# Transposes in 64x64 tiles for about half of the work, PSUM as four pairs for any step, output in halves, and no second loads

## The chip, the core and the metric

The kernel runs on one core of a Trainium2 chip. The metric is the device time of one execution in microseconds (us), as the median of several runs. Beside the timed runs there is one profiled execution; every duration below that is not a median comes from it. The engines are TensorE (PE, with its weight loads as PEld), VectorE (DVE), ScalarE (ACT), GpSimd (POOL) and SyncE (SP, which issues most DMAs).

## What is computed

Sigmoid attention over 8 batches, 12 heads, 448 positions and a head width of 64, and then a token-mixing MLP over the attention's output. The reference, cut to what matters:

```python
scores = scale * np.matmul(q, k.transpose(0, 1, 3, 2)) - np.log(S)     # S = 448
attn = 1.0 / (1.0 + np.exp(-scores))
attn_out = np.matmul(attn, v)                                         # [8, 12, 448, 64]
x = attn_out.transpose(0, 2, 1, 3).reshape(B, S, H * D)               # [8, 448, 768]
wq = x @ w_q                                                          # [8, 448, 64]
wk = x @ w_k
W_tok = 1/np.sqrt(64) * np.einsum('bsd,btd->bst', wq, wk)
mixed = np.einsum('bst,btd->bsd', W_tok, x)
out = np.maximum(mixed, 0.0) @ w_out                                  # [8, 448, 768]
```

All inputs and the output are float32; the kernel computes in bfloat16 with float32 accumulation.

## The kernel before

**The unit of work** is a quad: four heads of one batch, three quads to a batch, 24 in all. A quad's q, k and v (448 KB each) are loaded as [128 partitions, 2, 7*64]: a partition holds seven consecutive positions of a head, and `i` from 0 to 6 counts them. GpSimd casts them to bfloat16 (`cast1`, L131).

**Letters.** All work of PE after the start is written out as a string, `PLAN` (L464), one letter for a step; PE, and with it DVE and ACT, runs the steps in exactly this order. Each row of the string belongs to one quad's seven score steps.

- `q`, `k` (`tr`, L149): the transposition of a quad's q or k. For most quads PE does it: seven whole-array 128x128 transposes (L161) into one PSUM bank and a copy by DVE (L165). For quads 16 to 22 (`TWICE`) DVE does it with a 32x32 block transpose (L154). That needs another layout, for which `load1` (L107) loads most of the data twice, with four DMAs of 216 KB in place of one of 448 KB (tiles qb and kb).
- `S` (`scores`, L170): four 64x64 matmuls of 448 columns that run side by side in the array's four quarters, then one sigmoid of 128x896 on ACT (L179).
- `P` (`values`, L185): four 64x64 matmuls that add one seventh of the values to PSUM; after seven, DVE copies the result out (L201).
- `x` (`tr_x`, L206): eight whole-array transposes of the attention's output (L213) and a copy by DVE (L218).
- `W`, `N`, `U`, `M`: the mixing MLP of a batch. `W` (L228) is one of six matmuls with w_q and w_k; `N` (L244) four whole-array transposes; `U` (L252) eight 128x64 matmuls; `M` (L270) four 64x64 matmuls and a relu, on DVE, or on ACT for `m`.
- `O` (`out_chunk`, L292): six 128x128 matmuls of 384 columns that make half of an output block, and a copy on DVE, or on ACT for `o`; every second one issues the block's stores.
- `K`: the rest of the first quad's k.

**PSUM** has eight banks of 2 KB per partition. Three pairs of banks (`free2`) serve `S`, `P` and `M`; two single banks (`free1`) serve everything else. Each list is used first in, first out.

**Loads.** `ORDER` (L377) is the order in which SP issues the loads and GpSimd casts them. `pump_loads` (L394) issues a load when the buffer that it needs has been cast from (three buffers per tensor, two of the double kind), and `pump` (L409) casts when the cast's own buffer is free. The SP queue also carries the output's stores, in program order.

**The tail.** From the last score step on, what remains is 7 P, 6 W, 2 x, N, U, 6 M and 15 O; copies are then divided over DVE and ACT and stores over SP and ACT.

Of the kernel before, what the change touches and what calls it, by code (L numbers as in the profile page):

```python
# [16 lines left out]
def kernel(  # L17
# [19 lines left out]
    P = 128  # L37
# [27 lines left out]
    ps_f = pool("ps_f", 1, space=bass.MemoryType.PSUM)  # L65

    free2 = ["a", "b", "c"]
    free1 = ["d", "e"]

    def bank2(name):  # L70
        n = free2.pop(0)
        return n, ps_q.tile([P, 2, 512], F32, tag=n, name=name)

    def bank(shape, dtype, name):
        n = free1.pop(0)
        return n, ps_f.tile(shape, dtype, tag=n, name=name)
# [3 lines left out]
    wqk32 = singles.tile([P, NC, P], F32, name="wqk32")  # L80
# [4 lines left out]
    zeros = singles.tile([P, P], BF16)  # L85
# [16 lines left out]
    TWICE = {'q': (16, 17, 18, 19, 20, 21, 22), 'k': (16, 17, 18, 19, 20, 21, 22)}  # L102
# [3 lines left out]

    def load1(n, nm, eng):  # L107
        u, j = quads[n]
        if n in TWICE.get(nm, ()):
            t = p_lb.tile([P, 2, 14 * HD], F32, tag=nm + "b32", name=nm + "b32")  # L110
            for g in range(2):
                src = SRC[nm][u, 4 * j + 2 * g : 4 * j + 2 * g + 2].rearrange(
                    "h (p r) d -> p h (r d)", r=14
                )
                for dh in range(2):
                    r0 = 64 * g + 32 * dh
                    eng.dma_start(  # L117
                        out=t[r0 : r0 + 32, :, 0 : 13 * HD + 32],
                        in_=src[:, :, 32 * dh : 32 * dh + 13 * HD + 32],
                    )  # L120
        else:
            t = p_ld.tile([P, 2, NI * HD], F32, tag=nm + "32", name=nm + "32")
            eng.dma_start(  # L123
                out=t,
                in_=SRC[nm][u, 4 * j : 4 * j + 4].rearrange(
                    "(g h) (p i) d -> (h p) g (i d)", g=2, i=NI
                ),
            )
        ld[nm, n] = t

    def cast1(n, nm, eng):  # L131
        if n in TWICE.get(nm, ()):
# [5 lines left out]
        else:  # L138
            p = p_v16 if nm == "v" else p_c16
            t16 = p.tile([P, NI, 2, HD], BF16, tag=nm + "16", name=nm + "16")  # L140
            eng.tensor_copy(  # L141
                out=t16.rearrange("p i b d -> p b i d"),
                in_=ld.pop((nm, n)).rearrange("p b (i d) -> p b i d", i=NI),
            )
        ld[nm + "16", n] = t16

    qk = {}

    def tr(n, nm):  # L149
        t16 = ld.pop((nm + "16", n))  # L150
        t = p_qk.tile([P, 2, NI, NP], BF16, tag=nm + "t", name=nm + "t")
        qk[nm, n] = t
        if n in TWICE.get(nm, ()):
            nc.vector.transpose(  # L154
                out=t.rearrange("p h i n -> p (h i n)").bitcast(F32),
# [3 lines left out]
        fb, ps = bank([P, NI, 2, NP], BF16, "pt" + nm)  # L159
        for i in range(NI):  # L160
            nc.tensor.transpose(  # L161
                ps[:, i].rearrange("p h n -> p (h n)"),
                t16[:, i].rearrange("p b d -> p (b d)"), ident16,
            )
        nc.vector.tensor_copy(out=t, in_=ps.rearrange("p i h n -> p h i n"))  # L165
        free1.append(fb)
# [3 lines left out]
    def scores(n, i):  # L170
        fb, sc = bank2("sc")
        for g in range(2):
            for h in range(2):
                nc.tensor.matmul(  # L174
                    sc[HALF[h], g, 0:S], qk["k", n][HALF[g], h, i, :],
                    qk["q", n][HALF[g], h].rearrange("p i n -> p (i n)"), start=True, stop=True,
# [3 lines left out]
        free2.append(fb)  # L180
# [4 lines left out]
    def values(n, i, tail):  # L185
        u, j = quads[n]
        if i == 0:
            pv[n] = bank2("pv")
        fb, ps = pv[n]
# [6 lines left out]
        if i == NI - 1:  # L196
# [5 lines left out]
            free2.append(fb)  # L202
# [3 lines left out]
    def tr_x(n, tail):  # L206
# [3 lines left out]
        fb, ps = bank([P, 4, 2, 2, HD], BF16, "px")  # L210
        for h in range(2):
            for m in range(4):
                nc.tensor.transpose(  # L213
                    ps[:, m, :, h], xt(u, j)[:, h, m * P : (m + 1) * P], ident16
                )
        for g in range(2) if tail else (slice(0, 2),):
            w = slice(2 * j * P, 2 * (j + 1) * P) if not tail else slice((2 * j + g) * P, (2 * j + g + 1) * P)
            COPY["s" if tail and g else "v"](  # L218
                out=xns[u][:, :, w],
                in_=ps[:, :, g].rearrange("p m h d -> p m (h d)")  # L220
                if tail else ps.rearrange("p m g h d -> p m (g h d)"),
            )
        free1.append(fb)
# [4 lines left out]
    def mlp_wqk(u, c, tail):  # L228
        if c == 0:
            pw[u] = bank([P, S], F32, "pw")  # L230
        fb, ps = pw[u]
# [3 lines left out]
        if c == NC - 1:  # L235
# [6 lines left out]
            free1.append(fb)  # L242

    def mlp_wkn(u):  # L244
        fb, ps = bank([P, 4, P], BF16, "pk")
        for m in range(4):
            nc.tensor.transpose(ps[:, m], wqks[u % 2][:, m * P : (m + 1) * P], ident16)
        wkn[u] = p_one.tile([P, 4, DH], BF16, tag="wkn", name="wkn")
        nc.vector.tensor_copy(out=wkn[u], in_=ps[:, :, 64:128])
        free1.append(fb)  # L250

    def mlp_tmp(u, act):  # L252
        tmps[u] = p_one.tile([P, NB], BF16, tag="tmp", name="tmp")
        fb, ps = bank([P, NB], F32, "pt")
# [7 lines left out]
        free1.append(fb)  # L262
# [7 lines left out]
    def mlp_mix(u, c, act, tail):  # L270
        if c == 0 and u % 2 == 0:
            mxs[u // 2] = [p_mx.tile([P, 2, 2, S], BF16, tag=f"mx{n}", name="mx") for n in range(NC // 2)]
        fb, ps = bank2("pm")
# [13 lines left out]
        free2.append(fb)  # L287
# [3 lines left out]

    def out_chunk(act, tail):  # L292
        w, m, nb = chunks.pop(0)
        if nb == 0:
# [3 lines left out]
        def block(ps, w0, w1):  # L298
            for c in range(NC):
# [14 lines left out]
        fb, ps = bank([P, NB], F32, "po")  # L314
        if tail and w == NU // 2 - 1 and not chunks:
            h = NB // 2
            block(ps[:, 0:h], NB, NB + h)
            nc.vector.tensor_copy(out=o[:, NB : NB + h], in_=ps[:, 0:h])
            fb2, ps2 = bank2("po")
            block(ps2[:, 0, 0:h], NB + h, D)  # L320
            nc.scalar.copy(out=o[:, NB + h :], in_=ps2[:, 0, 0:h])
            store(slice(NB, NB + h))
            store(slice(NB + h, D))
            return
        block(ps, nb * NB, (nb + 1) * NB)
        COPY["s" if act else "v"](out=o[:, nb * NB : (nb + 1) * NB], in_=ps)  # L326
        free1.append(fb)
# [6 lines left out]
    def load_weights():  # L334
        for x, w in enumerate((moe_w_q, moe_w_k)):
            nc.sync.dma_start(
                out=wqk32[:, :, 64 * x : 64 * x + 64], in_=w.rearrange("(c p) n -> p c n", p=P)
# [20 lines left out]
    nc.vector.memset(zeros, 0.0)  # L358
    nc.vector.memset(bias_t, attn_bias)
    nc.gpsimd.memset(ident, 0.0)  # L360
# [6 lines left out]
    fb, ps = bank2("pwarm")  # L367
    for _ in range(32):
        nc.tensor.matmul(ps[:, 0, 0:P], zeros, zeros, start=True, stop=True)
    free2.append(fb)  # L370
    for t in xts:
        nc.vector.memset(t[:, :, S:], 0.0)
    for t in wqks:
# [4 lines left out]
        "v0 q1 k1 v1 k2 q2 q3 k3 q4 k4 v2 k5 k6 w0 k7 v3 "  # L378
        "w1 q5 q6 k8 v4 w2 q7 w3 v5 w4 k9 q8 v6 q9 w5 w6 "
        "v7 q10 k10 v8 v9 q11 k11 q12 v10 k12 v11 q13 k13 k14 q14 q15 "  # L380
        "v12 q16 k15 v13 v14 q17 k16 v15 k17 q18 k18 q19 v16 k19 v17 k20 "
        "k21 v18 v19 v20 v21 q20 q21 q22 v22 q23 k22 k23 v23 "
# [3 lines left out]
    BACK = {}  # L386
    for nm in "qkv":
        mine = {True: [], False: []}
        for n in range(N):
            kind = n in TWICE.get(nm, ())  # L390
            BACK[nm, n] = (kind, list(mine[kind]))
            mine[kind].append(n)

    def pump_loads():  # L394
        while len(loaded) < len(ORDER):
            nm, n = ORDER[len(loaded)]
            if nm == "w":
                if n >= 3 and ("w", n - 2) not in cast:
                    break
                load_wout(n - 1) if n else load_weights()  # L400
            else:
                kind, before = BACK[nm, n]
                back = 2 if kind else 3
# [154 lines left out]
```

## Time and profile before

| | us |
|---|---|
| median of 3 runs (205.08 to 206.51) | 205.62 |
| the profiled execution | 204.95 |
| its span, from the first to the last instruction | 203.2 |
| PE busy | 192.2 |
| ACT busy | 171.2 |
| DVE busy | 123.1 |
| POOL busy | 80.3 |
| sigmoids (L179), 168 of 1.016 | 156.1 busy |
| output matmuls (L300), 342 | 61.8 busy |
| DMA | 53.13 MB, mean 262 GB/s |
| loads of the double kind | 56 issues of 216 KB |

Busy time is the union of the instructions' spans. A matmul's span holds its way through the array, so that spans of following matmuls overlap; what a matmul costs is the distance to the start of the next. An engine's idle time costs nothing where another engine sets the pace. In a line of the profile `sc<-qt,kt` says that the tile sc is written from qt and kt, `128x896 bf16` are partitions, elements and type, and `x8` is the number of instructions merged into the line.

### The profile page before, as it was taken

To read this page: it belongs to the slowest core of one execution; us is meant where nothing else is said; L and a number is where in the kernel's file an instruction comes from. 1 tells how busy PE (TensorE), PEld (TensorE's weight loads), DVE (VectorE), ACT (ScalarE), POOL (GpSimd) and SP (SyncE) were. 2 spreads that over 40 slices of the span, in tenths; PEclk is the share of its full clock that TensorE was granted. 3 is DMA by queue.
4 is the path that set the end of the run, shared out by engine and by line. 5 is a ranking of instruction groups with operands and counts; after the bars stand their busy time and mean duration, and the time that the engine had idled before them with its cause. 6 is when DMAs were issued, how large, how long until landed. Compare 5 with 4: busy or idle time off the path is not lost.

```text
span 203.2 us, 5863 instructions
## 1 busy us (share of the span) xinstructions
PE 192.2 (95%) x2388; PEld 108.6 (53%) x2388; DVE 123.1 (61%) x196; ACT 171.2 (84%) x200; POOL 80.3 (40%) x95
## 2 busy tenths in 40 slices
PE   7669999999999999999999999999999899999991
PEld 7335545545556566555656555545455455555561
DVE  2226655866498567668777776858777654471230
ACT  4796999999989999889999999898998959974511
POOL 1577688676416624217642442511632600000000
PEclk9996999999999999999999999999999999999999
DMA  6999999899998999999999999999899933303575
GB/s 193 374 383 375 325 380 355 245 395 382 380 381 258 331 254 317 223 265 261 247 223 285 256 282 236 367 260 252 258 287 214 345 90 78 80 3 97 152 203 168
DMA packets 27786, 53.13 MB, mean 262 GB/s; under 512 B 4464, under 2 KB 19952, under 8 KB 27760
## 3 DMA queue, kind: packets, MB, share of 16 engines
q1 hardware_dynamic: 26960, 51.19, 85.9%
q10 hardware_dynamic: 800, 1.57, 2.1%
q8 instruction: 18, 0.29, 0.6%
q14 instruction: 8, 0.07, 0.1%
HBM read 41.75 MB, written 11.01 MB: 260 GB/s over the span
## 4 chain that ended last, share of the span: by engine, by line
DMA 41%; PE 31%; SPq 8%; ACT 8%; issue 4%; POOL 4%; DVE 1%; ACTq 1%; POOLq 0%
DMA qb<-in_q_dram 17%; DMA kb<-in_k_dram 12%; PE po L300 11%; PE sc L174 6%; ACT at L179 6%; SPq L117 5%; PE pv L192 5%; DMA q<-in_q_dram 4%; DMA out_dram<-o 4%; DMA v<-in_v_dram 4%; SPq L123 2%; PE pw L232 2%; PE ptk L161 2%; POOL k L134 2%; PE pt L257 2%
## 5 line engine op out<-in xcount | busy, mean ns | idle before, releaser
L179 ACT ACTIVATE at<-sc,bias_t 128x896 bf16<-128x896 f32 x168 | 156.1, 1016 | 13.6 <-PE sc L174 12.7
L300 PE MATMUL po<-wout,mx 128*128 128x384 bf16 (+1 forms) x342 | 61.8, 324 | 0.5 <-ACT o L326 0.3
L174 PE MATMUL sc<-qt,kt 64*64 64x448 bf16 x672 | 57.3, 363 | 2.4 <-DVE kt L451 1.0
L192 PE MATMUL pv<-at,v 64*64 64x448 bf16 x672 | 43.2, 353 | 0.7 <-POOL v L141 0.6
L300 PEld LDWEIGHTS <-mx 128*128 128x128 bf16 x342 | 30.9, 98 | 24.0 <-issue 7.0
L174 PEld LDWEIGHTS <-kt 64*64 64x64 bf16 x672 | 22.1, 104 | 24.3 <-issue 13.0
L201 DVE CAST xt<-pv 128x896 bf16<-128x896 f32 x23 | 25.0, 1088 | 16.1 <-PE pv L192 15.9
L326 DVE COPY o<-po 128x384 f32<-128x384 f32 x39 | 21.7, 556 | 16.9 <-PE po L300 11.8
L141 POOL CAST v<-v 128x896 bf16<-128x896 f32 x24 | 22.4, 934 | 15.2 <-PE pv L192 7.8
L268 DVE TENSOR_SCALAR mx<-pm 128x896 bf16<-128x896 f32 (+1 forms) x24 | 23.0, 969 | 7.2 <-PE pm L277 7.1
L192 PEld LDWEIGHTS <-v 64*64 64x64 bf16 x672 | 20.2, 107 | 12.3 <-issue 2.0
L218 DVE COPY xn<-px 128x1024 bf16<-128x1024 bf16 (+1 forms) x24 | 15.9, 663 | 7.3 <-PE px L213 7.2
L141 POOL CAST q<-q 128x896 bf16<-128x896 f32 x16 | 14.9, 933 | 9.9 <-DMA out_dram<-o 4.4
L141 POOL CAST k<-k 128x896 bf16<-128x896 f32 x16 | 14.9, 933 | 7.1 <-DMA k<-in_k_dram 4.3
L134 POOL CAST k<-kb 128x896 bf16<-128x896 f32 x7 | 8.3, 1192 | 19.4 <-DMA kb<-in_k_dram 9.2
L134 POOL CAST q<-qb 128x896 bf16<-128x896 f32 x7 | 8.2, 1190 | 18.3 <-issue 7.9
L213 PE MATMUL px<-ident,xt 128*128 128x128 bf16 x192 | 14.8, 220 | 0.1
L326 ACT COPY o<-po 128x384 f32<-128x384 f32 x16 | 7.7, 482 | 8.1 <-PE po L300 8.0
L213 PEld LDWEIGHTS <-xt 128*128 128x128 bf16 x192 | 11.5, 98 | 5.6 <-issue 4.8
L165 DVE COPY qt<-ptq 128x896 bf16<-128x896 bf16 x16 | 9.7, 618 | 7.1 <-PE ptq L161 7.0
L232 PE MATMUL pw<-xt,wqk 128*128 128x448 bf16 x48 | 13.8, 356 | 0.0
L165 DVE COPY kt<-ptk 128x896 bf16<-128x896 bf16 x16 | 9.9, 619 | 5.7 <-PE ptk L161 5.5
(53 smaller groups left out, 125.6 us busy)
## 6 DMA issues: line engine op xcount, KB each, us to landing
v<-in_v_dram SPq DMA_DIRECT2D x24, 448.0 KB, 7.8
out_dram<-o SPq DMA_DIRECT2D x47, 192.0 KB, 6.0
q<-in_q_dram SPq DMA_DIRECT2D x17, 448.0 KB, 7.5
k<-in_k_dram SPq DMA_DIRECT2D x16, 448.0 KB, 8.5
qb<-in_q_dram SPq DMA_DIRECT2D x28, 216.0 KB, 6.9
kb<-in_k_dram SPq DMA_DIRECT2D x28, 216.0 KB, 7.4
w<-in_moe_w_out_dram SPq DMA_DIRECT2D x6, 384.0 KB, 7.5
out_dram<-o ACTq DMA_DIRECT2D x7, 192.0 KB, 3.2
```

The lines of the kernel that those rows point to most:

```text
L134: eng.tensor_copy(out=t16.rearrange("p h i d y -> p h y i d"), in_=ld.pop((nm, n)).rearrange("p h (y i d) -> p h y i d", y=2, d=HD)[..., 0 ...
L141: eng.tensor_copy(out=t16.rearrange("p i b d -> p b i d"), in_=ld.pop((nm, n)).rearrange("p b (i d) -> p b i d", i=NI),)
L165: nc.vector.tensor_copy(out=t, in_=ps.rearrange("p i h n -> p h i n"))
L174: nc.tensor.matmul(sc[HALF[h], g, 0:S], qk["k", n][HALF[g], h, i, :], qk["q", n][HALF[g], h].rearrange("p i n -> p (i n)"), start=True, st ...
L179: nc.scalar.activation(at, sc[:, :, 0:S], ACTF.Sigmoid, bias=bias_t, scale=attn_scale)
L192: nc.tensor.matmul(ps[HALF[g], h, 0:S], ld["v16", n][HALF[h], i, g, :], ats[n, i][HALF[h], g, :], start=(i == 0), stop=(i == NI - 1),)
L201: nc.vector.tensor_copy(out=xt(u, j)[:, :, 0:S], in_=ps[:, :, 0:S])
L213: nc.tensor.transpose(ps[:, m, :, h], xt(u, j)[:, h, m * P : (m + 1) * P], ident16)
L232: nc.tensor.matmul(ps, wqk16[:, c, :], xt(u, c // 2)[:, c % 2, 0:S], start=(c == 0), stop=(c == NC - 1),)
L268: nc.vector.tensor_scalar(dst, ps, moe_scale, 0.0, ALU.mult, ALU.max)
L300: nc.tensor.matmul(ps, mxs[w][c % 3][:, c // 3].rearrange("p b s -> p (b s)")[:, m * P : (m + 1) * P], wout16[:, c, w0:w1], start=(c == 0) ...
L326: COPY["s" if act else "v"](out=o[:, nb * NB : (nb + 1) * NB], in_=ps)
```

## The change

- Every quad's q and k are transposed on PE. The letter now chooses how: `a` and `b` are the q and k of a quad in whole-array transposes as before (twelve quads, beside the first, whose start stays as it was); `q` and `k` are 28 transposes of 64x64 each, in seven groups of four that lie in the four quarters of the array (eleven quads). A quad's q and k go into one pair of PSUM banks and are copied out by one DVE instruction of 128x1792 after the second. The second loads and DVE's block transposes are no longer used.
- `X` is `tr_x` as before (ten times); `x` is 32 transposes of 64x64 (14 times). `N` is eight transposes of 64x64.
- PSUM is four pairs of banks. A step that needs one bank takes half of a pair, and the next such step the other half.
- `O` is now half of an output chunk: the first letter runs the first three of its six matmuls, the second the rest, the copy and the stores. In the last chunk each half is a block of 192 columns.
- `F`, 13 times near the start, is four 64x64 matmuls of 512 columns with zeros, whose result nothing reads.
- `PLAN` and `ORDER` are new. The small weights w_q and w_k are loaded into a w32 buffer, of which there are two, instead of one of their own, and the load of weight n waits for the cast of weight n-2 from n = 2 on.

The diff, cut to its core (`...` marks what is left out):

```diff
-    free2 = ["a", "b", "c"]
-    free1 = ["d", "e"]
...
+    pairs = [ps_q.tile([P, 2, 512], F32, tag=f"pp{n}", name=f"pp{n}") for n in range(4)]
+    pairs16 = [t.rearrange("p b x -> p (b x)").bitcast(BF16).rearrange("p (b x) -> p b x", b=2) for t in pairs]
+    free2 = [0, 1, 2, 3]
+    halves = []
+
+    def bank2():
         n = free2.pop(0)
+        return n, pairs[n], pairs16[n]
+
+    def bank1():
+        if halves:
+            n, b = halves.pop(0)
+        else:
+            n, b = free2.pop(0), 0
+            halves.append((n, 1))
+        return (n, b), pairs[n][:, b], pairs16[n][:, b]
+
+    def release(fb):
+        if isinstance(fb, int):
+            free2.append(fb)
+        elif (fb[0], 1 - fb[1]) in halves:
+            halves.remove((fb[0], 1 - fb[1]))
+            free2.append(fb[0])
+        else:
+            halves.append(fb)
...
-    TWICE = {'q': (16, 17, 18, 19, 20, 21, 22), 'k': (16, 17, 18, 19, 20, 21, 22)}
+    PLAN = (
+        "SFSFFSKFSSabPSPSPPFF",
+        "SFSPabSPSPaSbSFFPPSF",
+        "SXPPSPPPSaSbSFFFPSPPSab",
+        "SPPPPSXSSSWWXaWSbSWWW",
+        "SPPNSPPPSPPSabSaSbSU",
+        "SPPPMSPPSPPSabSXSXSPPPM",
+        "SPPPSPSWWWWMSXSWSSOWab",
+        "SOSqkSPPPSPPSoOSPPSoN",
+        "SSUOSPPxSPPPSPPSoOSPPM",
+        "SPPPSPPSWoOWMSSWWoMSWWoXSqPk",
+        "SPPPSPPPSOOSxSababSSOX",
+        "SPPPPSNPPPSUSOXSqkSOOSM",
+        "SoOSqkSoOSPPMSPPPSPPSoWWOW",
+        "SMSOOSSWWOWSSOOXONSqk",
+        "SUSqkPSPPPPSPPPSPPPSPPPSOO",
+        "SPPMSPPPPSPSWOOWSMSWoWOSM",
+        "SWOOSqkSoOSxSoWoPPNSPxPSPPP",
+        "SOOSxSoOSUSqkPSPPPSPPPP",
+        "SPPPSPPPSOOSxSoWOSxSoWWWo",
+        "SMSOWWSMOOOmqkSPPPPSPPPSoOSPxP",
+        "SPPPPSPSooONSxSUOSMSoOq",
+        "SkPSPPPPSPSPWooWWmMSOOqkSSWoWWO",
+        "SPxPSPPPPSSPoOOOSxSoooSPPPP",
+        "SNPPPSuxSSOoWoWMSSWoOWS",
+        "PPmPPPPPxmoWOWOoONxooUOoMmmoooOooOooOooOooOooooo",
+    )
+    KIND = ["a"] + [t for t in PLAN if t in "qac"]
...
+    def twice(nm, n):
+        return nm in "qk" and KIND[n] == "c"
...
+    def transposes(ps, t16, r):
+        for x, i in enumerate(range(r.start, r.stop)):
+            for g in range(2):
+                for h in range(2):
+                    nc.tensor.transpose(
+                        ps[HALF[g], h, x * NP : (x + 1) * NP], t16[HALF[h], i, g, :],
+                        ident16[HALF[h], HALF[h]],
+                    )
+    def transposes_whole(ps, t16, r):
+        for x, i in enumerate(range(r.start, r.stop)):
+            nc.tensor.transpose(
+                ps[:, x * P : (x + 1) * P], t16[:, i].rearrange("p b d -> p (b d)"), ident16,
             )
...
+        if t == 0:
+            ps_qk[n] = bank2()
+        fb, _, ps = ps_qk[n]
+        if kind in "ab":
+            transposes_whole(ps[:, t], t16, slice(0, NI))
+        else:
+            transposes(ps[:, :, t * S : (t + 1) * S], t16, slice(0, NI))
+        if t == 1:
+            qk[n] = p_qk.tile([P, 2, 2, NI, NP], BF16, tag="qk", name="qk")
...
+                nc.vector.tensor_copy(
+                    out=qk[n].rearrange("p t h i n -> p t h (i n)"),
+                    in_=ps[:, :, 0 : 2 * S].rearrange("p h (t x) -> p t h x", t=2),
+                )
+            release(fb)
...
+        fb, _, ps = bank2()
+        for m in range(4):
+            for h in range(2):
+                for g in range(2):
+                    for c in range(2):
+                        nc.tensor.transpose(
+                            ps[HALF[c], g, (2 * m + h) * HD : (2 * m + h + 1) * HD],
+                            xt(u, j)[HALF[g], h, (2 * m + c) * HD : (2 * m + c + 1) * HD],
+                            ident16[HALF[g], HALF[g]],
+                        )
...
         for m in range(4):
-            nc.tensor.transpose(ps[:, m], wqks[u % 2][:, m * P : (m + 1) * P], ident16)
+            for c in range(2):
+                nc.tensor.transpose(
+                    ps[HALF[c], m * DH : (m + 1) * DH],
+                    wqks[u % 2][HALF[1], (2 * m + c) * DH : (2 * m + c + 1) * DH],
+                    ident16[HALF[1], HALF[1]],
+                )
...
+        if opened:
+            w, m, nb, fb, ps = opened.pop()
+            part = 1
+        else:
+            w, m, nb = chunks.pop(0)
+            fb, ps, _ = bank1()
+            part = 0
...
+        block(ps, nb * NB, (nb + 1) * NB, part * NC // 2, (part + 1) * NC // 2)
+        if not part:
+            opened.append((w, m, nb, fb, ps))
+            return
...
+    nc.vector.memset(zeros[:, P:], 0.0)
...
-        "v0 q1 k1 v1 k2 q2 q3 k3 q4 k4 v2 k5 k6 w0 k7 v3 "
-        "w1 q5 q6 k8 v4 w2 q7 w3 v5 w4 k9 q8 v6 q9 w5 w6 "
...
+        "q1 k1 v0 k2 q2 v1 q3 k3 v2 q4 q5 k4 k5 v3 w0 q6 "
+        "k6 k7 q7 v4 k8 q8 v5 w1 q9 q10 k9 w2 k10 w3 w4 k11 "
...
-                if n >= 3 and ("w", n - 2) not in cast:
+                if n >= 2 and ("w", n - 2) not in cast:
...
+        if t == "F":
+            for g in range(2):
+                for h in range(2):
+                    nc.tensor.matmul(
+                        pairs[free2[0]][HALF[h], g], zeros[HALF[g], 0:64], zeros[HALF[g], :],
+                        start=True, stop=True,
+                    )
+            continue
```

## The prediction

> **What bounds the kernel now.** I read the page first, then the span cut into five stages at the instants where the score matmuls of quads 0, 2, 7 and the last one start. The columns of that second view are length, busy time of each engine (instructions in brackets), granted clock, DMA share and GB/s.
>
> ```profile
> PE 192.2 (95%) x2388; PEld 108.6 (53%) x2388; DVE 123.1 (61%) x196; ACT 171.2 (84%) x200; POOL 80.3 (40%) x95
> ...
> DMA 41%; PE 31%; SPq 8%; ACT 8%; issue 4%; POOL 4%; DVE 1%; ACTq 1%; POOLq 0%
> ```
>
> ```profile
> 0.00:6.38 6.38, 4.85 (x43) 4.32 (x44) 2.08 (x14) 2.57 (x4) 1.43 (x8) 1.00 0.71 226
> 6.38:21.61 15.23, 12.09 (x158) 6.39 (x161) 5.70 (x9) 12.65 (x14) 10.92 (x13) 0.89 1.06 373
> 21.61:53.17 31.56, 31.18 (x427) 16.80 (x419) 20.56 (x29) 31.24 (x36) 23.84 (x29) 1.00 1.00 351
> 53.17:176.26 123.09, 122.15 (x1586) 68.47 (x1584) 86.11 (x128) 112.74 (x126) 44.14 (x48) 1.00 0.94 258
> 176.26:203.20 26.94, 21.89 (x187) 12.60 (x186) 8.66 (x17) 11.97 (x24) 0.00 (x0) 1.00 0.46 120
> ```
>
> The chain in the first fence gives DMA 41%, but the stages contradict it as a limit: where the second loads run (53 to 176), PE is busy 122.15 of 123.09 us. DMA is nearly always in flight because loads are issued ahead; PE hardly waits for it. Below I call the stages opening, A (two quads), B (five), C (seventeen) and D (after the last scores).
>
> To price PE I use its timeline in the middle of C, taking start to start, since busy spans overlap.
>
> ```profile
> 107.36 0.57 PE L174 MATMUL sc<-qt,kt 64*64 64x448 bf16 x8
> 107.86 0.62 PE L213 MATMUL px<-ident,xt 128*128 128x128 bf16 x8
> 108.32 1.14 PE L300 MATMUL po<-wout,mx 128*128 128x384 bf16 x6
> 109.30 0.61 PE L213 MATMUL px<-ident,xt 128*128 128x128 bf16 x8
> 109.84 0.38 PE L174 MATMUL sc<-qt,kt 64*64 64x448 bf16 x4
> 110.05 0.35 PE L277 MATMUL pm<-wqk,tmp 64*64 64x448 bf16 x2
> 110.06 0.35 PE L277 MATMUL pm<-wq,tmp 64*64 64x448 bf16 x2
> 110.24 1.30 PE L192 MATMUL pv<-at,v 64*64 64x448 bf16 x24
> 111.39 0.38 PE L174 MATMUL sc<-qt,kt 64*64 64x448 bf16 x4
> ```
>
> Six groups of four 64x64 matmuls take 111.39 - 110.24 = 1.15 us: 0.19 a group (S, P or M). Six output matmuls take 0.98: 0.1625 each, 0.975 a chunk. Eight whole-array transposes take 108.32 - 107.86 = 0.46, of which about 0.01 is the entry, so 0.056 each. **Changing the array's mode costs**: two score groups before px take 0.50, not 0.38; eight transposes before sc take 0.54, not 0.45, and the first group after them 0.21, not 0.19. Either direction is about 0.115.
>
> ACT's own pace comes from its timeline:
>
> ```profile
> 20.26 21.66 ACT L179 ACTIVATE at<-sc,bias_t 128x896 bf16<-128x896 f32 x24 [0.51 <-PE sc L174]
> ```
>
> 24 sigmoids of 1.01 in 21.66 without a gap: (21.66 - 1.01)/23 = 0.898 each, 6.29 a quad. Stage B is five quads in 31.56, 6.31 each: **B is ACT's**. Stage C is 7.24 a quad, above ACT's pace, with PE full: **C is PE's**. For C I add up the plan of before by letters: 253 S, P and M at 0.189 is 47.8; 39 chunks 38.0; 30 W at 0.189 5.7; 16 x sets at 0.448 7.2; 16 q or k sets at 0.392 6.3 (the other 14 are on DVE); six U at 0.65 3.9; five N 1.1; together 110.0. The plan changes mode 102 times in C, 11.7. The sum is 121.7 against 123.09; 1.4 is waiting, 0.82 of it one wait for DVE kt L154 at 160.66. So the prices hold.
>
> Stage A loses time at the start of the data:
>
> ```profile
> 14.08 0.94 POOL q L141
> 15.07 0.56 PE ptq L161 x7
> ```
>
> In this piece of the chain quad 2's q is cast at 14.08, and PE, waiting in its fixed order, transposes it at 15.07; the clock granted in A is 0.89. Two quads take 15.23 where ACT needs 12.6.
>
> **The change, part by part.** *Tile transposes.* After the change 22 q or k sets (28 small transposes, seven groups of four), 14 x sets (32, eight groups) and all eight N (eight, four groups of two) are 64x64; 24 q or k sets and ten x sets stay whole. 294 of the groups lie in C and D. No row shows a 64x64 transpose, so bounds: from below, halving the columns of the whole transpose's 56 ns gives 28 ns for a group; the four weight loads of a group, exposed after a mode change, cost 0.21 - 0.19, some 20 to 25 ns together, so four do run side by side. From above, pv at 110.24 is 24 matmuls and 24 loads in 1.15, one PE instruction per 24 ns, and no merged stretch is much faster; eight instructions at that are 192 ns. I take 30 ns, nearest to the whole transpose with its columns halved, and because the two pm rows start 0.01 apart, which shows that a group is not issued at 24 ns each. The ends are 24 and 192 ns.
>
> The Trainium skill speaks against this twice. "TensorEngine Tiling (Array Packing)", Instruction Overhead, gives every matmul some 60 cycles and advises not to tile a dimension that is already small; as 25 ns for each of the four, an estimate from that page, a group would be 100 ns and the end some 20 us later. "TensorE: Matmul & The Clock Gate", LDWEIGHTS, divides columns by 1.2, which makes 53 ns of a 64-column load and the end some 7 us later, an estimate again; the 20 to 25 ns exposed after a mode change argue for less.
>
> *Stage C after, by letters:* 254 S, P and M 48.0; 81 halves at 0.4875 39.5; 34 W 6.4; four whole x 1.8; 12 tiled x at 0.24 2.9; four whole q or k sets 1.6; 22 tiled sets at 0.21 4.6; six U 3.9; six N 0.7; together 109.4. Mode changes fall from 102 to 97: 11.2. Sum 120.6. In a few plan rows ACT (6.29 plus its copies) exceeds PE, 0.7 more. Waiting was 1.4; without the wait for DVE kt it is some 0.5. C becomes 121.8, **1.3 shorter**. Note what it hides: the 14 sets that were on DVE come back to PE (14 x 0.39 = 5.5 if whole), and the cheaper tiles pay for them.
>
> *No second loads.* 56 DMA issues of 216 KB become 14 of 448 KB: 12.4 MB becomes 6.4, and 42 issues leave SP's queue. DVE loses 14 stream transposes of 0.63, POOL's casts fall from 1.19 to 0.93. All lie beside a full PE in C; the value is the 0.8 counted above, and if PE were not the cover it could be no more than C's 123.09 - 122.15 idle.
>
> *q and k share a PSUM pair and one copy.* 128x512 and 128x896 evacuations were 0.425 and 0.619, so 128x1792 is about 0.159 + 1792 x 0.513 ns = 1.08 us on DVE, against 1.24 for two. The k set's consumer, the scores of that quad, comes a quad or more later in the plan; DVE has 86 of 123 us used in C. Nothing, unless a pair is missing (rival two).
>
> *PSUM as four pairs.* Before, scores, values and mixes had three pairs, the rest two single banks. Now a value group holds a pair, an open W or output half another, a transpose set a third. I cost it at nothing: PE is behind ACT in C, so the previous sigmoid has usually freed its pair. The other bounds are rival two, and from below the 0.5 of waits left.
>
> *Output in halves.* The same six matmuls and one copy and store per chunk, in two steps; what it adds is mode changes, counted above.
>
> *Opening, fillers and order.* The extra memset (384 columns) ends before DVE's q cast at 4.20. Ten fillers of 0.21 in A are 2.1 us of PE; A's PE work becomes 10.2 under ACT's 12.6, and B's three leave B's at 30.0 under 31.4. In ORDER q1, k1 now precede v0, and q2 is the fifth load, one earlier. 448 KB at A's 373 GB/s is 1.23 us, so q2's cast comes at about 12.9 and its transposition at 13.9, while the plan asks for it one score step after quad 1 starts at 12.7. What is late next is k2 and q2 against PE, by some 0.4, and ACT has sigmoids in hand. The small weights now share the two w32 buffers, so w2's load waits on SP for w0's cast, which stands 13 places earlier in ORDER: nothing. A becomes 12.6 + 0.4 = 13.0, **2.2 shorter**; between nothing (rival three) and 2.6. B stays at 35 x 0.898 = 31.4, **0.1 shorter**.
>
> *Stage D.* Its two x sets go to tiles (-0.4), four of six W move into C (-0.8, counted there), a mix goes (-0.2): 20.8 of PE becomes 19.3; the 6.1 of waits and of copying and storing the last block stays. 25.4, **1.5 shorter**.
>
> Sum: 6.4 + 13.0 + 31.4 + 121.8 + 25.4 = 198.0 of span. The profiled execution was 204.95 with a span of 203.2, so 1.75 lies around it: 199.8. It stood 0.67 under the median of the runs, so **200.4** as a median.
>
> **Rivals.** *One, slower: PE takes the many small instructions one after another.* Mechanism: a 64x64 set is 56 or 64 PE instructions with nothing long to hide their issue. It decides from 30 + 5.2/0.294 = 48 ns a group, where the gain is gone. For it: one instruction per 24 ns is the fastest sustained pace shown. Against: pm's two rows. At 60 to 80 ns, 209 to 215; at 192 ns 248.
>
> *Two: a pair is missing.* Where values, an open half and a transpose set hold three pairs, the next scores wait for the sigmoid before them. A score step is then 0.35 + 1.01 = 1.36 instead of C's mean 1.03, 0.33 lost at up to 25 tiled sets: 8 us at all, half of that at half of them: 204 to 208. PE runs in its written order, so values, output halves and the next transposes queue behind that score group, and ACT waits for it. For it: a sigmoid holds its pair for 1.01. Against: ACT idles 10 of 123 us in C, so it is seldom behind.
>
> *Three: the start is set by DMA, not by order.* A's DMA share is 1.06 at 373 GB/s, full either way; if A stays at 15.2, 202.6.
>
> *Four: the tiles do what they should, but ACT keeps C.* Its 112.7 busy in C is a floor well below 121.8; it gives at most 1 us, within the forecast's range.
>
> **How the numbers follow.** Forecast 0.50, own range 197.5 to 203; rival one 0.27; rival two 0.13; rival three and four 0.10. About 1% (2 us) is what a measurement of this kernel can tell from no change, so 203.5 and 207.7 are the borders. Faster: the forecast and half of the last case, less a little, 0.53; within 1%: most of rival two and the mild end of rival one, 0.19; slower: 0.28. The range leaves out the far part of rival one: 197 to 212.
>
> **What would show it.** Right: tiled sets start to start near 0.21 and 0.24 us; quad 2's scores near 19.5; C near 122 with PE full; mode changes fewer by some 20. Wrong: a tiled set of over 0.35 us; waits of PE on ACT at score groups after q, k or x; quad 2 still near 21.6. A set price over 48 ns a group turns the sign.

## The result, and the profile after

The changed kernel takes **219.17 us** (median of four runs, 217.69 to 220.74) against 205.35 (205.0 to 206.51) for the kernel before, run beside it: ratio **1.066**, 95% interval 1.056 to 1.077. The prediction was 200.4 us, in a range of 197 to 212, with 0.53 for faster. The sign was wrong and the time lies outside the range. Ratios here and below are formed from fast executions alone, that is without those over 1.5% above the fastest of their kernel, while each time given is the median of all of them.

The busy times of the page, and how the chain of work divides over the engines:

```profile
PE 193.9 (89%) x3368; PEld 111.6 (51%) x3368; DVE 122.2 (56%) x171; ACT 173.0 (79%) x202; POOL 76.8 (35%) x95
...
PE 56%; DMA 21%; DVE 6%; POOL 4%; issue 4%; ACT 3%; SPq 3%; ACTq 1%; DVEq 0%; POOLq 0%
```

PE is busy for 193.9 us, 1.7 more than before, in a span that is 15.3 longer. So PE didn't get slower: it stands still. The chain hints at one thing that it waits for: DVE, 1% of it before, has 6%, some 13 us. (That PE's own share has gone from 31% to 56% says nothing of waiting.) The stages, cut where the scores of quads 0, 2, 7 and the last ones start (length, busy time of PE, PE's weight loads, DVE, ACT and POOL, granted clock, DMA share, GB/s):

```profile
0.00:5.92 5.92, 4.48 (x44) 4.07 (x44) 2.29 (x15) 2.57 (x4) 1.20 (x7) 1.00 0.68 192
5.92:21.39 15.47, 12.55 (x178) 6.85 (x182) 4.74 (x5) 12.04 (x14) 9.95 (x11) 0.89 1.04 377
21.39:54.62 33.23, 31.68 (x477) 18.79 (x469) 21.13 (x24) 32.54 (x37) 23.80 (x29) 1.00 0.92 308
54.62:191.29 136.67, 124.79 (x2451) 70.08 (x2449) 85.77 (x111) 115.36 (x129) 41.80 (x49) 1.00 0.61 197
191.29:218.50 27.21, 20.37 (x231) 11.81 (x230) 8.31 (x16) 10.53 (x21) 0.00 (x0) 0.96 0.43 117
```

Of the 15.3 us, 13.6 are in stage C (136.67 against 123.09), 1.7 in B; A has not become shorter (15.47 against 15.23). In C, PE was busy 122.15 of 123.09 before, and now leaves 11.9 us of 136.67 idle. What it waits for, as the list of waits of PE alone has it (engine and line that waits, who ends the wait: us in all, times, longest):

```profile
PE pp L339 <- DVE o L452: 3.4, 5, 0.7
PE pp L422 <- DVE wqk L344: 3.2, 5, 1.1
PE pp L422 <- DVE tmp L374: 2.5, 4, 0.7
PE pp L207 <- POOL q L193: 1.8, 1, 1.8
PE pp L215 <- POOL k L562: 1.6, 1, 1.6
PE pp L339 <- ACT o L452: 1.4, 2, 0.8
PE pp L339 <- DVE xn L303: 1.2, 2, 0.8
```

Five of these seven make no sense as data. L339 is a W step: it multiplies xt with the weights and needs nothing from `o`, the output chunk that DVE copies out at L452. L422 is the output and needs nothing from `wqk` of the other unit or from `tmp`. The two sides share only the name `pp`, a pair of PSUM banks. Here is one such place in PE's timeline (start, duration, what; in brackets the idle time before it and who ended it), with the two DVE instructions in question behind it:

```profile
71.70 1.14 PE L422 MATMUL pp<-wout,mx 128*128 128x384 bf16 x6
73.55 0.35 PE L339 MATMUL pp<-xt,wqk 128*128 128x448 bf16 x1 [0.72 <-DVE o L452]
73.83 0.38 PE L390 MATMUL pp<-wqk,tmp 64*64 64x448 bf16 x2
...
76.00 0.55 PE L339 MATMUL pp<-xt,wqk 128*128 128x448 bf16 x2
77.61 0.65 PE L422 MATMUL pp<-wout,mx 128*128 128x384 bf16 x3 [1.05 <-DVE wqk L344]
78.09 0.61 PE L298 MATMUL pp<-ident,xt 128*128 128x128 bf16 x8
78.63 0.38 PE L257 MATMUL pp<-qk 64*64 64x448 bf16 x4
78.85 0.39 PE L207 MATMUL pp<-ident,q 64*64 64x64 bf16 x28
79.06 0.37 PE L275 MATMUL pp<-at,v 64*64 64x448 bf16 x4
```

```profile
72.94 0.56 DVE L452 COPY o<-pp 128x384 f32<-128x384 f32 x1 [0.56 <-PE pp L422]
...
76.94 0.61 DVE L344 CAST wqk<-pp 128x448 bf16<-128x448 f32 x1
```

At 73.55 a W step begins the moment the copy of the output block ends (72.94 + 0.56), though it writes the other bank of that pair; at 77.61 an output half begins when the copy of `wqk` ends (76.94 + 0.61), again in the other bank. Matching every wait of PE in the program with the instruction that ends it, and taking what exceeds the usual distance between two starts, I find 22 waits of this kind, **15.5 us**; 20 waits for a reader of the same bank, 5.2 us; and 5.4 us of others, 1.8 of it for `POOL q` and most of the rest in the first 15 us. The same sum for the kernel before was 9.4 us, 1.7 of it between 28 and 176 us.

The theory after this reading: `bank1` hands out `pairs[n][:, b]`, a slice of one tile of two banks. The program orders accesses by tile, so that a write to one half waits for the copy that reads the other half. The rival was the prediction's rival two: pairs are too few, and the halves only show it.

### The profile page after: what moved, and what is told of

Same layout as the page of the kernel before. It is cut to its first block, busy times and chain, and to the rows that moved or that the text cites. A ratio compares the mean times of both kernels' runs of the same rounds, so it can differ in the third digit from the quotient of the medians.

```text
span 218.5 us, 7799 instructions
## 1 busy us (share of the span) xinstructions
PE 193.9 (89%) x3368; PEld 111.6 (51%) x3368; DVE 122.2 (56%) x171; ACT 173.0 (79%) x202; POOL 76.8 (35%) x95
## 4 chain that ended last, share of the span: by engine, by line
PE 56%; DMA 21%; DVE 6%; POOL 4%; issue 4%; ACT 3%; SPq 3%; ACTq 1%; DVEq 0%; POOLq 0%
PE pp L422 23%; PE pp L257 10%; PE pp L275 9%; DMA k<-in_k_dram 8%; DMA q<-in_q_dram 7%; DMA v<-in_v_dram 5%; PE pp L339 3%; PE pp L207 2%; PE pp L370 2%; PE pp L390 2%; SPq L174 2%; DVE wqk L344 2%; POOL q L193 2%; DVE o L452 2%; PE pp L315 1%
## 5 line engine op out<-in xcount | busy, mean ns | idle before, releaser
L262 ACT ACTIVATE at<-pp,bias_t 128x896 bf16<-128x896 f32 x168 | 156.0, 1012 | 22.0 <-PE pp L257 20.8
L422 PE MATMUL pp<-wout,mx 128*128 128x384 bf16 (+1 forms) x342 | 64.3, 324 | 7.1 <-DVE wqk L344 3.2
L257 PE MATMUL pp<-qk 64*64 64x448 bf16 x672 | 62.4, 363 | 0.9 <-DVE qk L571 0.6
L422 PEld LDWEIGHTS <-mx 128*128 128x128 bf16 x342 | 30.8, 97 | 34.6 <-issue 18.1
L275 PE MATMUL pp<-at,v 64*64 64x448 bf16 x672 | 46.3, 355 | 0.3 <-POOL v L193 0.3
L257 PEld LDWEIGHTS <-qk 64*64 64x64 bf16 x672 | 23.6, 105 | 25.5 <-issue 17.6
L452 DVE COPY o<-pp 128x384 f32<-128x384 f32 x38 | 21.2, 557 | 20.4 <-PE pp L422 17.1
L284 DVE CAST xt<-pp 128x896 bf16<-128x896 f32 x23 | 25.1, 1092 | 9.6 <-PE pp L275 9.4
L381 DVE TENSOR_SCALAR mx<-pp 128x896 bf16<-128x896 f32 (+1 forms) x22 | 21.5, 984 | 13.5 <-PE pp L390 13.5
L339 PE MATMUL pp<-xt,wqk 128*128 128x448 bf16 x48 | 14.5, 354 | 6.2 <-DVE o L452 3.4
L240 DVE COPY qk<-pp 128x1792 bf16<-128x1792 bf16 x12 | 13.0, 1091 | 11.8 <-PE pp L215 11.8
L245 DVE COPY qk<-pp 128x1792 bf16<-128x1792 bf16 x11 | 12.0, 1091 | 4.5 <-PE pp L207 4.4
L452 ACT COPY o<-pp 128x384 f32<-128x384 f32 x17 | 8.1, 481 | 6.9 <-PE pp L422 6.0
```

Source lines behind the costliest of these rows:

```text
L240: nc.vector.tensor_copy(out=qk[n].rearrange("p t h i n -> p t i h n"), in_=ps[:, :, 0 : 2 * S].rearrange("p t (i h n) -> p t i h n", i=NI, ...
L245: nc.vector.tensor_copy(out=qk[n].rearrange("p t h i n -> p t h (i n)"), in_=ps[:, :, 0 : 2 * S].rearrange("p h (t x) -> p t h x", t=2),)
L257: nc.tensor.matmul(sc[HALF[h], g, 0:S], qk[n][HALF[g], 1, h, i, :], qk[n][HALF[g], 0, h].rearrange("p i n -> p (i n)"), start=True, stop=True,
L262: nc.scalar.activation(at, sc[:, :, 0:S], ACTF.Sigmoid, bias=bias_t, scale=attn_scale)
L275: nc.tensor.matmul(ps[HALF[g], h, 0:S], ld["v16", n][HALF[h], i, g, :], ats[n, i][HALF[h], g, :], start=(i == 0), stop=(i == NI - 1),)
L284: nc.vector.tensor_copy(out=xt(u, j)[:, :, 0:S], in_=ps[:, :, 0:S])
```

## The experiments

**No sharing of pairs.** A step that needs one bank takes a pair for itself.

```diff
     def bank1():
-        if halves:
-            n, b = halves.pop(0)
-        else:
-            n, b = free2.pop(0), 0
-            halves.append((n, 1))
-        return (n, b), pairs[n][:, b], pairs16[n][:, b]
+        n = free2.pop(0)
+        return n, pairs[n][:, 0], pairs16[n][:, 0]
```

> The changed kernel, but a step that needs one bank takes a whole pair and no two steps ever share one. In the changed kernel's profile 22 PE waits end with a DVE or ACT read of the other bank of the pair that PE is about to write; they add up to 15.5 us beyond the pace of back-to-back matmuls. Theory one (the two banks of a pair are one tile to the dependencies, so PE waits for a read that does not concern its bank): these waits go and the time falls by 11 to 16, from 219 to 203 to 208. Theory two (a pair is missing when scores are due): more pairs are now held, so the time stays at 219 or rises.

Measured: 220.13 us, ratio 1.077 (1.070 to 1.084) to the kernel before. The waits for the other bank fell from 15.5 to 1.6 us, and the waits for a reader of the same bank rose from 5.2 (20 of them) to 21.0 (65). The list of PE's waits now has the sigmoid in it, in its first row:

```profile
PE pp L412 <- ACT at L252: 4.1, 10, 0.6
```

So without sharing, rival two takes over at the same price: the two explanations are not told apart by this, but it shows that the plan can't do without shared pairs. The time came out where the expectation had put theory two.

**Three pairs and two single banks**, the numbers of the kernel before, under the new plan:

```diff
-    pairs = [ps_q.tile([P, 2, 512], F32, tag=f"pp{n}", name=f"pp{n}") for n in range(4)]
+    pairs = [ps_q.tile([P, 2, 512], F32, tag=f"pp{n}", name=f"pp{n}") for n in range(3)]
+    ones = [ps_q.tile([P, 512], F32, tag=f"po{n}", name=f"po{n}") for n in range(2)]
...
     def bank1():
+        n = free1.pop(0)
+        return (n, 1), ones[n], ones16[n]
```

> The changed kernel, but PSUM is three pairs and two single banks that are tiles of their own; plan, transposes, halves of the output and loads are as changed. Theory one (false waits between the halves of a pair): 202 to 207, as no bank shares a tile with another step's. Theory two (too few pairs): worse than 219, since one pair fewer serves scores, values, mixes and tiled transposes.

Measured: 226.2 us, ratio 1.108 (1.100 to 1.116). False waits are gone (0.35 us), and waits for the same bank make 25.2 us, most of them scores that wait for a sigmoid. A likely reason is that a transposition of q and k now holds a whole pair between its two letters while one pair fewer is there; this was not tested by itself. The time again fits the expectation of theory two, so this was no repair and, with a pair less, no fair test of theory one.

**The kernel before, with its two single banks as the halves of one tile.** Nothing else is changed, so that the effect is alone:

```diff
+    both = ps_f.tile([P, 2, 512], F32, tag="de", name="de")
...
     def bank(shape, dtype, name):
         n = free1.pop(0)
-        return n, ps_f.tile(shape, dtype, tag=n, name=name)
+        size = math.prod(shape[1:])
+        t = (both if dtype == F32 else both16)[:, "de".index(n), 0:size]
...
+        return n, t
```

> The kernel before with its two single banks made the two halves of one tile; nothing else is changed. Theory one: every step in one of the banks now waits for the copy out of the other; some 130 such waits enter the program. At the 0.3 to 0.7 us that such a wait costs in the changed kernel, the time rises from 205 to between 225 and 290. Theory two (banks of one tile are independent): 205 as before.

Measured: **271.44 us**, ratio 1.329 (1.321 to 1.337). PE's waits go from 9.4 to 76.2 us. A piece of its timeline, `de` being the joined tile:

```profile
99.77 1.15 PE L311 MATMUL de<-wout,mx 128*128 128x384 bf16 x6
101.57 0.38 PE L258 MATMUL de<-ident,wqk 128*128 128x128 bf16 x4 [0.65 <-DVE o L337]
...
102.58 0.62 PE L224 MATMUL de<-ident,xt 128*128 128x128 bf16 x8
103.98 1.14 PE L311 MATMUL de<-wout,mx 128*128 128x384 bf16 x6 [0.78 <-DVE xn L229]
105.77 0.55 PE L172 MATMUL de<-ident,k 128*128 128x128 bf16 x7 [0.65 <-DVE o L337]
```

Each step that writes `de` waits for the copy of the step before, which lies in the other bank; matmul and copy, which overlapped, now alternate. That two banks in one tile wait for each other is thereby shown, in a kernel that has no small transposes, no new plan and no missing pair.

**v0 first.** The changed kernel with the load order `v0 q1 k1 k2 q2 v1 ...` in place of `q1 k1 v0 k2 q2 v1 ...`.

> The changed kernel with quad 0's v loaded and cast first again, ahead of q1 and k1, as before the change. The first quad took 9.6 us after the change and 6.3 before; its second part of k landed 2 us later. If the new order of the first loads did this, the time falls by 2 to 3 to 216 or 217; if not, it stays within 1 of 219, or rises by up to 1.2, one load's time, as q1 and k1 come later.

Measured: 218.15 us, ratio 1.067 (1.060 to 1.074), the same as the changed kernel. In the profile quad 0's row is 8.15 us instead of 9.63 and quad 7's 6.21 instead of 7.87; quad 1's is 6.49 instead of 5.85, and all other rows agree within some hundredths. The order of the first loads moves a microsecond or two at the start, and the sign of the result doesn't hang on it. PE's wait for quad 11's q in quad 7's row is not there in this execution.

**Independent halves.** The changed kernel with the false order removed: each write into one half is declared not to depend on the reads of the other half. Banks, plan and all instructions stay the same.

```diff
+    def mm(fb, i):
+        if not isinstance(fb, int):
+            tc.declare_no_dep(i.ins, group=f"half{fb[0]}{1 - fb[1]}", reason="other bank")
+
+    def rd(fb, i):
+        if not isinstance(fb, int):
+            tc.add_to_no_dep_group(f"half{fb[0]}{fb[1]}", i.ins)
...
-        nc.tensor.matmul(
+        mm(fb, nc.tensor.matmul(
...
-            nc.vector.tensor_copy(out=w[:, 0:S], in_=ps)
+            rd(fb, nc.vector.tensor_copy(out=w[:, 0:S], in_=ps))
```

> The changed kernel, with one thing altered: the program no longer makes an instruction that writes one bank of a pair wait for the copy that reads the other bank of that pair (the banks are handed out in the same order, and writes still wait for reads of their own bank). If the false waits between the halves are the loss, the 15.5 us of them in the changed kernel's trace go, at most a third of it comes back as waits for the same bank or for the sigmoids, and the time is 204 to 210. If the pairs themselves are too few (rival two of the prediction), as the run without any sharing of pairs suggested, the waits only move to the sigmoids and the time stays at 216 to 221. Four tiled transposes should still take 31 to 32 ns.

Measured: **205.32 us**, ratio 1.003 (1.000 to 1.006) to the kernel before. Some 13 of the 14 us are gone, and 15 of span in the profiled executions (218.5 to 203.6). The same place of the program as above:

```profile
69.47 1.14 PE L430 MATMUL pp<-wout,mx 128*128 128x384 bf16 x6
70.44 0.35 PE L347 MATMUL pp<-xt,wqk 128*128 128x448 bf16 x1
70.73 0.38 PE L398 MATMUL pp<-wqk,tmp 64*64 64x448 bf16 x2
...
72.90 0.55 PE L347 MATMUL pp<-xt,wqk 128*128 128x448 bf16 x2
73.28 0.65 PE L430 MATMUL pp<-wout,mx 128*128 128x384 bf16 x3
```

From the output to the W step it is 0.97 us, six matmuls at their own pace, where it was 1.85; from the W step at 72.90 to the output half 0.38, where it was 1.61. All other waits together grew by nothing: by the same matching, PE's waits fell from 26.1 to 10.4 us, of which waits for the same bank are 5.2 in both. **The false order between halves is the cause of the loss**, and rival two, which the first experiment had left possible, is not: the four pairs suffice as they are shared.

**Whole-array q and k in place of the tiles**, on top of independent halves (`"".join(PLAN).replace("q", "a").replace("k", "b")`).

> The kernel with independent halves, and the 22 tiled q and k sets made whole-array transposes again (same pairs, same order, same copies in number). It prices the tiles by their absence. By the rows (0.392 us for a whole set, 0.217 for a tiled one at 31 ns a group of four, and 22 more mode changes at 0.115) TensorE gets 3.9 + 2.5 = 6.4 us more work; where TensorE is the bound that is 5 to 7 us over the kernel with independent halves. If small transposes were no cheaper than whole ones, only the mode changes would remain: 1 to 3 us. If TensorE is not the bound there: 0 to 1 us.

Measured: 212.01 us, ratio 1.037 (1.030 to 1.044), 6.7 us over the kernel with independent halves. Part of that, 1.7 us, is a longer wait in quad 7's row, which the tiles have no part in. In the quads from 8 on, where PE is full in both, it is 121.90 against 117.04: 4.9 us for 20 sets and the mode changes around them, 5.8 by my prices. That is what the tiles are worth.

**The kernel before without second loads** (`TWICE = {}`): its 14 sets go back from DVE to PE, as whole-array transposes.

> The kernel before, with only one part of the change: no second loads, so that the 14 q and k sets that VectorE transposed are whole-array transposes on TensorE. By the prediction's prices TensorE gets 14 x 0.392 = 5.5 us and 12 mode changes more (1.4 us), and one wait of 0.8 us for VectorE may go: 205.4 + 6 = 210 to 213. If the second loads cost the kernel something that the trace doesn't show (queue, DMA, VectorE), less than that: 204 to 209.

Measured: 213.37 us, ratio 1.042 (1.035 to 1.049). Stage C is 131.6 instead of 123.1: 8.5 us, where 6.9 are PE's work by the prices, and the rest, some 2, are new waits for a copy of q or k to free one of the two single banks. This part of the change, alone, costs; it is the tiles that pay for it. Both together, with independent halves, come out at nothing, which is the 1.003.

**Scores first.** With independent halves the time is 205.3, still 5 over the forecast, so stage A was next. In the first row of the plan, quad 0's last two score groups stand behind quad 1's transposes and the first values, and these wait for loads. The edit puts them ahead, on top of independent halves:

```diff
-        "SFSFFSKFSSabPSPSPPFF",
+        "SFSFFSKFSSSSabPPPPFF",
```

> The kernel with independent halves, and its first plan row altered: quad 0's last two score groups are issued ahead of quad 1's transposes and of the first values (SFSFFSKFSSSSabPPPPFF in place of SFSFFSKFSSabPSPSPPFF). In the trace of the kernel with independent halves TensorE waits 0.9 for quad 1's q, 0.8 for its k and 0.7 us for v0 with those two score groups queued behind, and ScalarE runs dry. If this order is what kept stages opening and A at their old length, the two quads take 13 to 13.6 us instead of 15.2 and the time falls by 1.3 to 2.2 us. If the landing of the loads sets the start (rival three of the prediction), quad 2's scores stay at 21 to 21.6 us and the time within 0.5 us of the kernel with independent halves.

Measured: 205.24 us, ratio 1.002 (0.998 to 1.006): no gain. The start did become shorter (stage A 14.17 instead of 15.23), and it was given back in quad 7's row, which takes 10.15 us instead of 7.46 (this profiled execution is 1.5 us above the kernel's median, so that the size of this loss in a usual one isn't shown):

```profile
53.09 0.38 PE L265 MATMUL pp<-qk 64*64 64x448 bf16 x4
55.97 0.45 PE L215 MATMUL pp<-ident,q 64*64 64x64 bf16 x28 [2.50 <-POOL q L201]
```

PE waits there 2.5 us for POOL's cast of quad 11's q. SyncE's queue, in the same execution, shows why this q is late (time at which an issue starts, how long it takes or waits, and what is loaded):

```profile
38.45 4.92 SPq L478 DMA_DIRECT2D w<-in_moe_w_out_dram  x2
...
45.21 2.20 SPq L478 DMA_DIRECT2D w<-in_moe_w_out_dram  x2
47.46 1.56 SPq L182 DMA_DIRECT2D v<-in_v_dram  x1
49.07 0.46 SPq L182 DMA_DIRECT2D q<-in_q_dram  x1
```

An issue that waits for nothing takes 0.4 to 0.5 us here; the weights wait for a free buffer, and the q stands behind them in the queue.

**Three weight buffers**, on top of that:

```diff
-    p_w32 = pool("w32", 2)
+    p_w32 = pool("w32", 3)
...
-                if n >= 2 and ("w", n - 2) not in cast:
+                if n >= 3 and ("w", n - 3) not in cast:
```

> The kernel of the run before it (independent halves, scores first), with three buffers for the fp32 weights instead of two, as many as the big weights had in the kernel before together with a buffer of their own for the small ones. In the traces after the change SyncE waits 4.9 us at 38.8 and 2.2 us at 45.5 for a weight buffer, with q, k and v loads queued behind it, and in quad 7's row TensorE waits 1.4 to 2.0 us for a q that these loads bring. If the shared buffers are the cause, that wait goes and the time falls by another 1.2 to 1.8 us. If the loads are late because the DMA engines are full, the wait stays and the time with it.

Measured: **202.93 us**, ratio **0.994** (0.991 to 0.998): 7% under the changed kernel by the ratios, and 0.6% under the kernel before, a small gain whose interval ends just short of 1. The weights still wait on the queue, 3.43 and 2.46 us for the same two pairs of issues, but from 34.56 on instead of 38.45; so the q is issued at 45.20 instead of 49.07, the wait in quad 7's row is gone (6.11 us), and the gain at the start comes through. In stage A 0.7 us of the difference to the run before is an earlier landing of q1, for which the buffers have no part. Stages A, B, C and D:

```profile
6.07:19.53 13.46, 11.23 (x179) 6.38 (x182) 4.70 (x5) 12.24 (x14) 9.53 (x11) 1.00 1.05 382
19.53:51.51 31.98, 31.60 (x478) 18.86 (x470) 21.12 (x24) 31.95 (x36) 24.91 (x31) 1.00 1.02 354
51.51:174.66 123.15, 122.98 (x2450) 69.89 (x2449) 85.13 (x111) 114.92 (x129) 41.04 (x48) 1.00 0.66 212
174.66:200.20 25.54, 20.29 (x231) 11.90 (x230) 8.65 (x17) 10.90 (x22) 0.00 (x0) 0.98 0.49 134
```

C is full again, 122.98 of 123.15.

**No fillers**, on top of that: all 13 `F` taken out of the plan.

> The kernel of the run before it, without the 13 filler groups of the first three plan rows. I counted them as 2.7 us of TensorE work under ScalarE's pace in stages A and B, so at nothing. If that holds: within 0.5 us of the run before it. If they keep the granted clock up (it falls to 0.50 for some 3 us around 13 us in all kernels after the change), the clock should fall earlier or for longer and the time rise by 0.5 to 2 us.

Measured: 203.56 us, ratio 0.996 (0.992 to 0.999). The intervals of this and the run before overlap, so that 0.6 us is a hint and no more. In the profile PE's granted clock is at 0.50 from about 8 to 14 us and quad 2 starts at 21.00, where with the fillers the clock stays at 1.00 and quad 2 starts at 19.53. But q1's cast came 1.28 us later in this execution (8.73 against 7.45), which is nearly all of the 1.44 us by which A is longer. Nor do the fillers decide about the clock: all 13 are in the changed kernel, whose clock fell to 0.50 at 11.69, and there are none in the kernel before without second loads, whose clock stayed at 1.00. The first line is this run's, the second that kernel's:

```profile
8.00:14.00 6.00, 5.45 (x54) 3.09 (x58) 1.51 (x2) 5.04 (x6) 4.13 (x5) 0.50 1.05 388
4.00:14.00 10.00, 6.94 (x94) 3.39 (x91) 2.88 (x6) 8.50 (x11) 6.01 (x8) 1.00 1.04 366
```

The expectation's "in all kernels after the change" doesn't hold either: with three pairs and two single banks, and the same fillers, the clock stayed at 1.00 as well. What the fillers are worth is open.

## Why the prediction was wrong, point by point

**PSUM as four pairs: this is the step that failed.** It was costed "at nothing: PE is behind ACT in C, so the previous sigmoid has usually freed its pair". That argument is about how many pairs there are, and as to that it held: waits for the same bank are 5.2 us. It didn't ask what one pair is. The diff shows it: before, `ps_f.tile` gave each single bank a tile of its own; after, `bank1` returns a slice of a tile of two banks. The missing term is 15.5 us of waits in the trace, and 13 of the 14 us in the medians between the changed kernel and the one with independent halves. My rival two asked the neighbouring question and had 0.13; none of the rivals had this mechanism. By stages, the profiled span of 218.5 lies 20.5 above the sum of 198.0: 14.9 in C, 2.5 in A, 1.8 each in B and D, less 0.5 in the opening.

**The tiles: right.** I took 30 ns for a group of four, with ends at 24 and 192. The median over some 200 groups followed by one of the same kind is 32, the quarters lie at 31 and 32; in the lines above, 28 transposes take 79.06 - 78.85 = 0.21 us. So rival one, my likeliest way to lose, is refuted. The Trainium skill, "TensorEngine Tiling (Array Packing)", Instruction Overhead, has about 60 cycles for each matmul; the estimate from it was 100 ns a group, and the measurement is a third of that. "TensorE: Matmul & The Clock Gate", LDWEIGHTS, from which the other estimate of 53 ns came, is too high here as well. 171 mode changes became 152, some 20 fewer as predicted. The one copy of 128x1792 took 1.09 us, for which the sum had 1.08.

**Stage C: the terms were right, the waits weren't.** The sum was 120.6 of work and 0.5 of waits. With halves independent and the weights in time, C is 123.15, 1.1% over the 121.8. The changed kernel's 136.67 is, within a microsecond or so, this plus the false waits that lie in C and the late q.

**No second loads: right.** The loads were hidden, as argued from a PE that is full in C; the 5.5 us for the sets that return to PE were, with their mode changes, 6.9 counted and 8.5 measured in the kernel before.

**Small weights in a shared buffer, "nothing": wrong by some 2 us where it was tested** (205.24 to 202.93 with a third buffer). I had looked at w2's wait for w0's cast alone. The ring of two delays every later weight too, and w5 and w6 stand in the queue ahead of quad 11's q. In the changed kernel it is the wait of 1.8 us for `POOL q` in the list above; that the weights cause it was shown only on top of independent halves. Over the profiles with two buffers PE's wait lies between none (no sharing, three pairs and two singles, v0 first) and 3.05 us (whole q and k), though SyncE waits for a buffer in all of them (4.90 and 1.93 us with v0 first, 4.85 and 2.07 in the changed kernel). So two buffers cost something only where this q lands after PE needs it.

**Stage A, "2.2 shorter": two things were missed.** It was 15.47. The first is the order on PE: I had quad 1 start at 12.7 from ScalarE's pace, and had not followed that quad 0's last two scores queue behind k1 and v0. The second is that the loads don't land at a fixed time: q1's cast, the first after quad 0's, began between 7.45 and 9.47 in the profiles of kernels with the same load order, and q2's, for which I had 12.9, between 12.30 and 14.39. Where q1 was cast at 8.19 (whole q and k) and 8.14 (scores first), A took 15.14 and 14.17, so the order of those letters is worth about 1.0 us, by one execution each; between the runs with scores first, q1's cast at 8.14 and 7.45 goes with A at 14.17 and 13.46, microsecond for microsecond. Rival three said that the data set the start: half right.

**Stages B and D.** D was to be 25.4 and is 25.58 with independent halves; B 31.4 and 31.98. The remaining distance of the best version to the forecast, 202.02 against 199.8 in profiled executions, is 1.35 in C and about half a microsecond each in A and B, less 0.3 in the opening; its causes were not followed up.

The range held the sum of known costs and no term for what the diff does to order. It reached 212 for rival one; a wrong sign by a mechanism outside all rivals had no place in it.

## What to carry to other kernels

When a change puts two buffers into one tile, price the waits between them: list for each half who reads it last, and add a copy's length wherever the other half is written meanwhile; if the banks are really apart, give them tiles of their own or declare the independence. When the profile after shows a wait between two instructions that share no data, look at what they share by name. And when a start is sped up, look for the next queue that has not moved, here the weight loads, before counting the gain.

## What the runs showed of the hardware

**Four 64x64 transposes side by side take 31 to 32 ns**, their weight loads included, over sets of 28 and 32. One whole 128x128 transpose, which moves the same amount, takes 56, 1.75 times as long. So eight PE instructions fit into 32 ns, and the fastest long stretch of the kernel before, one instruction per 24 ns, was no limit of issue.

**The granted clock fell to half after short idle times.** Four rows of the changed kernel, cut as the stages above were, but 1 us long:

```profile
7.00:8.00 1.00, 0.33 (x8) 0.00 (x0) 0.00 (x0) 1.00 (x2) 0.00 (x0) 1.00 1.01 372
8.00:9.00 1.00, 0.08 (x2) 0.08 (x3) 0.00 (x0) 1.00 (x2) 0.61 (x1) 1.00 1.05 403
...
11.00:12.00 1.00, 0.35 (x5) 0.33 (x5) 0.00 (x0) 1.00 (x2) 0.73 (x2) 0.85 1.07 385
12.00:13.00 1.00, 0.73 (x10) 0.46 (x12) 0.29 (x1) 0.17 (x1) 0.82 (x1) 0.50 1.04 375
```

PE is busy 0.33 and 0.08 us of these two microseconds, the longest single wait is 1.59, and some 3 us later the clock is at 0.50, for 3 us, though PE is then busy. The Trainium skill, "TensorE: Matmul & The Clock Gate", HAM oscillation, warns of idle gaps over about 3.4 us; no gap here is half as long, and the clock fell all the same. Short gaps don't always do it: in the kernel before without second loads PE was busy for 6.94 of the 10 us from 4 to 14, in the changed kernel for 6.81, and there the clock stayed at 1.00. What decides is not shown here.
